# First product of the token groups in seven block products of eight, as the second one is, in a fused state space and PReLU kernel

## The chip, the cores and the metric

One core of a Trainium2 chip runs one program. The metric is the device time of one execution in microseconds (us), taken as the median over several executions. "Before" was run again beside every set of experiments, on the same chip: its medians were 415.87 to 416.51 us, except for the last set (415.48).

Engine names in the profile: PE is the matrix engine (TensorE), PEld its weight loads, DVE the VectorE, ACT the ScalarE, POOL the GpSimd.

## The reference

The first half is a state space scan over chunks of tokens; the second half, on which the change works, is two dense products with a PReLU between them.

```
def _moe_ref(x, w_in, w_out, alpha):
    h = x @ w_in                                         # 3072x256 @ 256x2048
    g = np.maximum(h, 0.0) + alpha * np.minimum(h, 0.0)
    return (g @ w_out).astype(np.float32)                # 3072x2048 @ 2048x256

def reference(**kwargs):
    ...                                                  # state space part, chunk by chunk
    attn_out = _attn_ref(**attn_kwargs)                  # (4, 8, 768, 32)
    x = np.ascontiguousarray(attn_out.transpose(0, 2, 1, 3)).reshape(B * S, H * D)
    return _moe_ref(x=x, **moe_kwargs)
```

All is float32. In the profile one float32 matmul leaves two records.

## The kernel before

Tokens go in six groups of 512. Group 0 is worked off with the weight loading; groups 1 to 5 form the main loop. The 2048 hidden units are 16 tiles of 128. For each tile, `hidden` multiplies 512 tokens by the two halves of the input and makes the PReLU from the PSUM bank: ScalarE writes `alpha*h`, VectorE takes the maximum with `h`.

```
def hidden(g, f, t0, nt):
    ...
    for k in range(KC):                                  # KC = 2
        nc.tensor.matmul(hp, w_in[:, k, f * P : (f + 1) * P], xts[g][:, k, t0 : t0 + nt],
                         start=(k == 0), stop=(k == KC - 1))
    gt = gts[g, f][:, t0 : t0 + nt]
    nc.scalar.mul(gt, hp, s_alpha[:, f : f + 1])
    nc.vector.scalar_tensor_tensor(out=gt, in0=hp, scalar=s_mul[:, f : f + 1], in1=gt,
                                   op0=ALU.mult, op1=ALU.max)
```

The second product is already in seven block products of eight (a Strassen-Winograd scheme). GpSimd makes the four differences of hidden blocks (`hidden_sums`, 256 elements each), TensorE runs the seven products into four banks (`products`), and one group later `combine` adds the seven results up:

```
def combine(g):
    ...
    nc.vector.tensor_tensor(out=c[0][:, 0], in0=m[2], in1=sa[:, 0], op=ALU.add)
    nc.vector.tensor_tensor(out=u[:, 0], in0=m[6], in1=sa[:, 0], op=ALU.add)
    nc.vector.tensor_tensor(out=u[:, 1], in0=m[7], in1=u[:, 0], op=ALU.add)
    nc.gpsimd.tensor_tensor(out=u4[:, 0], in0=u[:, 0], in1=sa[:, 1], op=ALU.add)
    ...
    nc.vector.tensor_tensor(out=c[0][:, 1], in0=m[3], in1=u4[:, 0], op=ALU.add)
```

The state space part is a generator, `pair`, whose steps are spread between the tiles. Its pieces:

```
bn = pair_loads(gp)                     # GpSimd: B times the decays, wanted by the state update
...
nc.vector.tensor_tensor_scan(out=dv[:, k], data0=abc[k], data1=ident_h, ...)   # 1024 elements
...
# state update: TensorE bn x xt, then VectorE `state`, GpSimd `sm`
for k in range(2):                      # gram products: two ss banks each, freed by VectorE masks
    gram = [ss_tile() ... for r in range(2)]
    ... nc.tensor.matmul(gram[r], bh[rs, k], cz[rs, :, k], ...)
    ... nc.vector.tensor_tensor(out=dec[:, k, hs], in0=gram[r], in1=dec[:, k, hs], op=ALU.mult)
    yield
```

The main loop goes through pairs of tiles; `products` run two pairs behind `hidden`.

Of the kernel before, what the change touches and what calls it, by code (L numbers as in the profile page):

```python
# [9 lines left out]
F32 = mybir.dt.float32  # L10
U32 = mybir.dt.uint32
U16 = mybir.dt.uint16
ALU = mybir.AluOpType
# [9 lines left out]
def kernel(  # L23
# [21 lines left out]


    nc = tc.nc
    ctx.enter_context(tc.manual_schedule(engines={
# [5 lines left out]
    P = 128  # L54
    Q = 128
    CPB = S // Q
    R = S // P
    NCH = batch * CPB
    HD = H * D
    RW = batch // 2 * H * CPB  # L60
    d_model, d_ff = moe_w_in.shape
    KC = d_model // P
    NF = d_ff // P
    GC = 4
    GT = GC * Q
    NG = NCH // GC
    NP = NCH // 2
    LAG = 2
    NQ = NF // 2
    HM = d_model // 2  # L70
    HT = GT // 2
    NB = 2
    WQ = 256
    assert H * N == P and HD == d_model and KC == 2 and R == CPB == 6
    assert NCH % GC == 0 and GT == 512 and NF % 2 == 0 and d_model <= WQ

# [4 lines left out]
    wld = ctx.enter_context(tc.tile_pool(name="wld", bufs=6))  # L81
    wtp = ctx.enter_context(tc.tile_pool(name="wtp", bufs=2))
    lda = ctx.enter_context(tc.tile_pool(name="lda", bufs=3))
    ldx = ctx.enter_context(tc.tile_pool(name="ldx", bufs=3))
    work = ctx.enter_context(tc.tile_pool(name="work", bufs=2))
    xtp = ctx.enter_context(tc.tile_pool(name="xtp", bufs=2))
    gp = ctx.enter_context(tc.tile_pool(name="gp", bufs=16))
# [179 lines left out]
    xts = {}  # L267
# [80 lines left out]
    def pair(gp):  # L348
# [7 lines left out]
        def decays(k):  # L356
# [5 lines left out]
            for w, t in enumerate(ahead.pop(k, None) or spread(z, k)):  # L362
                ws = slice(512 * w, 512 * w + 512)
                nc.vector.tensor_tensor_scan(out=dv[:, k, ws], data0=t, data1=ident_h[:, ws],  # L364
                                             initial=0.0, op0=ALU.mult, op1=ALU.add)

        ahead = {}
        if not abc:
# [28 lines left out]
        nc.scalar.copy(out=bh.rearrange("p k t -> p (k t)"), in_=tp[:, : 2 * P])  # L397
        cz = work.tile([P, 4, 2, Q], F32, name="cz")
        for e in range(4):
            nc.scalar.mul(cz[:, e].rearrange("p k t -> p (k t)"), ct, par[:, e : e + 1])  # L400
        if gp == 0:
# [6 lines left out]

        if gp:
            decays(0)  # L410
            yield
            decays(1)
# [27 lines left out]
        masked[b] = st[-1]  # L440
        yield


# [56 lines left out]

    def output(f):

        if f == 0:
            pos[0] = [bank(i).rearrange("p (t m) -> p t m", t=2) for i in range(GC // 2)]
        gt = gts.pop((0, f))
        for t in range(GC):
            nc.tensor.matmul(pos[0][t // 2][:, t % 2], gt[:, t * Q : (t + 1) * Q], w_out[:, f],  # L507
                             start=(f == 0 and t % 2 == 0), stop=(f == NF - 1),
                             skip_group_check=True)
        if f == NF - 1:  # L510
            for i, po in enumerate(pos.pop(0)):
                o_sb = op.tile([P, 2, d_model], F32, name="o_sb")
                nc.scalar.copy(out=o_sb, in_=po)
                t0 = 2 * i * Q
                nc.sync.dma_start(
                    out=out[t0 : t0 + 2 * Q, :].rearrange("(s p) m -> p s m", p=Q), in_=o_sb)
# [3 lines left out]
    wq = w_out.rearrange("p (q j) (i m) -> p q j i m", j=2, i=2)  # L520
    sums = []

    def weight_sums(q):
        if not sums:
            sums.extend(wld.tile([P, NQ, HM], F32, name=f"ws{i}", tag="raw") for i in range(3))
        a11, a12, a21, a22 = wq[:, q, 0, 0], wq[:, q, 1, 0], wq[:, q, 0, 1], wq[:, q, 1, 1]
        s1, s2, s4 = (t[:, q] for t in sums)
        for o, x0, x1, f in ((s1, a21, a22, ALU.add), (s2, s1, a11, ALU.subtract),
                             (s4, a12, s2, ALU.subtract), (a21, a11, a21, ALU.subtract)):
            nc.gpsimd.tensor_tensor(out=o, in0=x0, in1=x1, op=f)  # L530

    tsums = {}

    def hidden_sums(g, q):

        b11, b12 = (gts[g, 2 * q][:, h * HT : (h + 1) * HT] for h in range(2))
        b21, b22 = (gts[g, 2 * q + 1][:, h * HT : (h + 1) * HT] for h in range(2))
        ta = gp.tile([P, 2, HT], F32, name="gt")
        tb = gp.tile([P, 2, HT], F32, name="gt")
        t1, t3, t2, t4 = ta[:, 0], ta[:, 1], tb[:, 0], tb[:, 1]  # L540
        for o, x0, x1 in ((t1, b12, b11), (t3, b22, b12), (t2, b22, t1), (t4, t2, b21)):
            nc.gpsimd.tensor_tensor(out=o, in0=x0, in1=x1, op=ALU.subtract)  # L542
        s1, s2, s4 = (t[:, q] for t in sums)

        tsums[g, q] = [(1, wq[:, q, 0, 0], b11), (2, wq[:, q, 1, 0], b21), (6, s2, t2),
                       (5, s1, t1), (7, wq[:, q, 0, 1], t3), (4, wq[:, q, 1, 1], t4), (3, s4, b22)]

    ms = {}
    HALVES = {1: (0, 0), 2: (0, 1), 6: (1, 0), 7: (1, 1), 4: (2, 0), 3: (2, 1), 5: (3, 0)}

    def products(g, q, which):
        if q == 0 and which[0] == 0:
            ms[g] = [bank(i).rearrange("p (h t) -> p h t", h=2) for i in range(4)]
        for j in which:
            n, w, b = tsums[g, q][j]
            i, h = HALVES[n]
            nc.tensor.matmul(ms[g][i][:, h], w, b, start=(q == 0 and h == 0),  # L557
                             stop=(q == NQ - 1), skip_group_check=True)

    ends_of = {}  # L560

    def combine(g):

        m = {n: ms[g][i][:, h] for n, (i, h) in HALVES.items()}
        sa = wtp.tile([P, 2, HT], F32, name="sa", tag="wt")
        u = wtp.tile([P, 2, HT], F32, name="u", tag="wg")
        u4 = wtp.tile([P, 2, HT], F32, name="u4", tag="wr")
        c = [work.tile([P, 2, HT], F32, name=f"c{i}") for i in range(2)]
        last = g == NG - 1
        engs = [nc.sync, nc.scalar]  # L570
        nc.scalar.copy(out=sa[:, 0], in_=m[1])
        nc.scalar.copy(out=sa[:, 1], in_=m[5])
        nc.vector.tensor_tensor(out=c[0][:, 0], in0=m[2], in1=sa[:, 0], op=ALU.add)
        nc.vector.tensor_tensor(out=u[:, 0], in0=m[6], in1=sa[:, 0], op=ALU.add)
        nc.vector.tensor_tensor(out=u[:, 1], in0=m[7], in1=u[:, 0], op=ALU.add)
        nc.gpsimd.tensor_tensor(out=u4[:, 0], in0=u[:, 0], in1=sa[:, 1], op=ALU.add)
        nc.vector.tensor_tensor(out=c[1][:, 0], in0=u[:, 1], in1=m[4], op=ALU.subtract)
        nc.gpsimd.tensor_tensor(out=c[1][:, 1], in0=u[:, 1], in1=sa[:, 1], op=ALU.add)
        if last:
            turn(g, 0, c[0], slice(0, HT), engs)  # L580
            turn(g, 1, c[1], slice(0, GT), engs)
        nc.vector.tensor_tensor(out=c[0][:, 1], in0=m[3], in1=u4[:, 0], op=ALU.add)
        ms.pop(g)
        if last:
            turn(g, 0, c[0], slice(HT, GT), engs)
        else:
            ends_of[g] = c
# [12 lines left out]

    def finish(g):
        for i, c in enumerate(ends_of.pop(g)):
            turn(g, i, c, slice(0, GT), [nc.sync])

    pairs = {}

    def ssm(gp, stages=1):

        if gp not in pairs:
            pairs[gp] = pair(gp)  # L610
        for i in range(stages):
            next(pairs[gp], None)
# [5 lines left out]
    for i in range(3, 6):  # L618
# [10 lines left out]
    second = {0: (2, 1), 1: (2, 1), 2: (2, 1), 3: (2, 1), 5: (2, 1), 6: (3, 1), 7: (3, 1),  # L629
              8: (3, 1), 9: (3, 1), 11: (3, 1), 13: (3, 1)}  # L630
    for n in range(2):
        for f in range(NF):
# [15 lines left out]
            if n and f >= LAG:  # L648
                output(f - LAG)
    early[0] = None  # L650

    steps = {0: (1, 1), 1: (1, 1), 2: (1, 0), 3: (1, 0), 4: (1, 1), 5: (1, 1), 6: (1, 0), 7: (1, 0)}
    for i in range(NQ * (NG - 1)):
        g, q = divmod(NQ + i, NQ)
        nxt = 2 * g + 2 + q // 4
        if q % 4 == 0 and nxt < NP:
            if nxt == 4:
                load_rows(1)
                held["pr"] = rows_scan(1)
                rows_out(1)  # L660
            if nxt + 1 < NP:
                load_pair(nxt + 1)
        if i < NQ:
            weight_sums(i)
        for j in range(2):
            if steps[q][j] and nxt < NP:
                ssm(nxt)
            hidden(g, 2 * q + j, 0, GT)
            if i == 0:
                output(NF - LAG + j)  # L670
            elif i >= LAG:
                products(*divmod(NQ + i - LAG, NQ), range(4) if j == 0 else range(4, 7))
        hidden_sums(g, q)
        if g > 1 and q == LAG - 1:
            combine(g - 1)
        if g > 1 and q == LAG:
            finish(g - 1)

    for q, which in ((6, (0,)), (7, (0,)), (6, (1,)), (7, (1,)), (6, (3,)), (7, (3,)),
                     (6, (2, 4, 5)), (7, (2, 4, 5)), (6, (6,)), (7, (6,))):  # L680
        products(NG - 1, q, which)
    combine(NG - 1)


# [28 lines left out]
```

## Time and profile before

The four runs of the kernel before gave 415.72 to 416.1 us. A "wait" below is idle time of TensorE that the profile puts down to another engine. In the table, the granted clock is the share of full speed that TensorE got, averaged over the profiled execution.

| | before |
|---|---|
| median time | 415.96 us |
| profiled span | 413.6 us |
| TensorE busy | 392.2 us (95%) |
| VectorE, ScalarE, GpSimd busy | 212.6, 124.0, 216.7 us |
| mean granted clock | 0.994 |
| share of PE in the chain that ended last | 85% |

### The profile page before, as it was taken

To read this page: it belongs to the slowest core of one execution; us is meant where nothing else is said; L and a number is where in the kernel's file an instruction comes from. 1 tells how busy PE (TensorE), PEld (TensorE's weight loads), DVE (VectorE), ACT (ScalarE), POOL (GpSimd) and SP (SyncE) were. 2 spreads that over 40 slices of the span, in tenths; PEclk is the share of its full clock that TensorE was granted. 3 is DMA by queue.
4 is the path that set the end of the run, shared out by engine and by line. 5 is a ranking of instruction groups with operands and counts; after the bars stand their busy time and mean duration, and the time that the engine had idled before them with its cause. 6 is when DMAs were issued, how large, how long until landed. Compare 5 with 4: busy or idle time off the path is not lost.

```text
span 413.6 us, 5226 instructions
## 1 busy us (share of the span) xinstructions
PE 392.2 (95%) x1891; PEld 251.1 (61%) x1891; DVE 212.6 (51%) x322; ACT 124.0 (30%) x248; POOL 216.7 (52%) x267
## 2 busy tenths in 40 slices
PE   5878789999999999999999999999999999999993
PEld 4454558778556566566566566556556556666672
DVE  5999893852833732762732752731852731252223
ACT  3564824413223114124114124114123112221120
POOL 3244673450786965754734744734744824363441
PEclk9999999999999999999999999999999999999997
DMA  9939994100960610107810106920102000011003
GB/s 214 256 102 236 292 213 91 56 2 10 219 113 0 122 45 0 52 0 117 182 33 2 51 0 103 174 56 0 51 2 52 2 1 0 2 22 30 0 2 51
DMA packets 124122, 30.53 MB, mean 74 GB/s; under 512 B 96880, under 2 KB 120000, under 8 KB 124096
## 3 DMA queue, kind: packets, MB, share of 16 engines
q1 hardware_dynamic: 117792, 29.67, 32.1%
q10 hardware_dynamic: 6304, 0.52, 1.1%
q8 instruction: 15, 0.25, 0.2%
q14 instruction: 11, 0.09, 0.1%
HBM read 26.85 MB, written 3.34 MB: 73 GB/s over the span
## 4 chain that ended last, share of the span: by engine, by line
PE 85%; DVE 8%; POOL 3%; ACT 1%; DMA 1%; issue 1%; POOLq 0%; DVEq 0%
PE hp L494 37%; PE bank L557 28%; PE bank L507 7%; PE ss L448 5%; PE ss L471 2%; DVE dec L364 2%; DVE wr L221 1%; DVE dec L453 1%; PE ss L393 1%; PE ss L464 1%; PE ss L422 1%; DVE gt L498 1%; PE bank L342 1%; DVE dec L359 1%; DMA ap<-in_a_dram 1%
## 5 line engine op out<-in xcount | busy, mean ns | idle before, releaser
L542 POOL TENSOR_TENSOR gt<-gt 128x256 f32<-128x256 f32 x160 | 143.0, 905 | 140.5 <-DVE gt L498 118.7
L494 PE MATMUL hp<-xT,w_in 128*128 128x512 f32 (+1 forms) x416 | 179.4, 554 | 4.4 <-DVE gt L498 4.3
L498 DVE SCALAR_TENSOR_TENSOR gt<-hp,s_mul,gt 128x512 f32<-128x512 f32 (+1 forms) x104 | 71.4, 687 | 144.2 <-ACT gt L497 144.2
L497 ACT ACTIVATE gt<-hp,s_alpha 128x512 f32<-128x512 f32 (+1 forms) x104 | 66.7, 641 | 222.6 <-PE hp L494 185.8
L494 PEld LDWEIGHTS hp<-xT,w_in 128*128 128x128 f32 x416 | 74.8, 190 | 66.4 <-issue 53.3
L557 PEld LDWEIGHTS bank<-gt,w_out 128*128 128x128 f32 x320 | 60.8, 190 | 40.7 <-issue 36.1
L557 PE MATMUL bank<-gt,w_out 128*128 128x256 f32 x320 | 82.0, 379 | 0.0
L557 PE MATMUL bank<-gt,ws 128*128 128x256 f32 x240 | 64.7, 379 | 0.0
L557 PEld LDWEIGHTS bank<-gt,ws 128*128 128x128 f32 x240 | 45.6, 190 | 6.2
L359 DVE TENSOR_TENSOR_SCAN dec<-abc,ident_h 128x1024 f32<-128x1024 f32 x20 | 47.9, 2395 | 0.0
L453 DVE TENSOR_TENSOR dec<-ss,dec 128x512 f32<-128x512 f32 x40 | 25.7, 684 | 12.0 <-PE ss L448 12.0
L507 PE MATMUL bank<-w_out,gt 128*128 128x256 f32 x128 | 30.2, 379 | 0.0
L507 PEld LDWEIGHTS bank<-w_out,gt 128*128 128x128 f32 x128 | 24.3, 190 | 4.2 <-issue 1.0
L448 PE MATMUL ss<-cz,bh 64*128 64x512 f32 x80 | 24.3, 640 | 0.4 <-DVE cd L406 0.4
L224 POOL TENSOR_TENSOR w_out<-wr,wg 128x512 uint32<-128x512 uint32 x8 | 13.9, 1736 | 11.7 <-DVE wr L221 9.1
L400 ACT ACTIVATE cz<-ss,par 128x256 f32<-128x256 f32 x48 | 18.9, 484 | 0.0
L224 POOL TENSOR_TENSOR w_in<-wr,wg 128x512 uint32<-128x512 uint32 x7 | 8.9, 1272 | 13.6 <-DVE wr L221 13.6
L406 DVE TENSOR_TENSOR cd<-ss,ap 128x256 f32<-128x256 f32 x10 | 4.2, 424 | 20.1 <-ACT cz L400 20.1
L195 POOL TENSOR_SCALAR wt<-wt 128x512 f32<-128x512 f32 x15 | 11.3, 751 | 5.9 <-ACT wt L193 4.8
L437 POOL TENSOR_TENSOR sm<-state,bmask 128x256 f32<-128x256 f32 (+1 forms) x12 | 7.6, 637 | 10.4 <-DVE state L433 10.4
L448 PEld LDWEIGHTS ss<-cz,bh 64*128 64x128 f32 x80 | 6.9, 184 | 10.0 <-issue 6.1
L221 DVE SCALAR_TENSOR_TENSOR wr<-wt,wr 128x512 uint32<-128x512 uint32 x16 | 11.1, 693 | 2.4 <-POOL wt L195 1.0
(92 smaller groups left out, 249.3 us busy)
## 6 DMA issues: line engine op xcount, KB each, us to landing
abc<-z SPq DMA_DIRECT2D x20, 512.0 KB
raw<-in_moe_w_in_dram SPq DMA_DIRECT2D x8, 512.0 KB
raw<-in_moe_w_out_dram SPq DMA_DIRECT2D x8, 512.0 KB
xt<-in_x_dram SPq DMA_DIRECT2D x24, 128.0 KB
out_dram<-o_sb SPq DMA_DIRECT2D x34, 64.0 KB
nat<-in_B_dram SPq DMA_DIRECT2D x22, 64.0 KB
nat<-in_C_dram SPq DMA_DIRECT2D x22, 64.0 KB
ap<-pf SPq DMA_DIRECT2D x10, 128.0 KB
```

The source lines that it names most:

```text
L221: nc.vector.scalar_tensor_tensor(out=r, in0=t, scalar=3, in1=r, op0=ALU.logical_shift_left, op1=ALU.bitwise_xor)
L224: add.tensor_tensor(out=d, in0=r, in1=g.bitcast(U32), op=ALU.add)
L359: nc.vector.tensor_tensor_scan(out=dv[:, k], data0=abc[k], data1=ident_h, initial=0.0, op0=ALU.mult, op1=ALU.add)
L400: nc.scalar.mul(cz[:, e].rearrange("p k t -> p (k t)"), ct, par[:, e : e + 1])
L448: nc.tensor.matmul(gram[r].rearrange("p h t -> p (h t)"), bh[rs, k], cz[rs, :, k], start=True, stop=True, tile_position=(64 * r, 0), skip_ ...
L453: nc.vector.tensor_tensor(out=dec[:, k, hs], in0=gram[r], in1=dec[:, k, hs], op=ALU.mult)
L494: nc.tensor.matmul(hp, w_in[:, k, f * P : (f + 1) * P], xts[g][:, k, t0 : t0 + nt], start=(k == 0), stop=(k == KC - 1))
L497: nc.scalar.mul(gt, hp, s_alpha[:, f : f + 1])
L498: nc.vector.scalar_tensor_tensor(out=gt, in0=hp, scalar=s_mul[:, f : f + 1], in1=gt, op0=ALU.mult, op1=ALU.max)
L507: nc.tensor.matmul(pos[0][t // 2][:, t % 2], gt[:, t * Q : (t + 1) * Q], w_out[:, f], start=(f == 0 and t % 2 == 0), stop=(f == NF - 1), s ...
L542: nc.gpsimd.tensor_tensor(out=o, in0=x0, in1=x1, op=ALU.subtract)
L557: nc.tensor.matmul(ms[g][i][:, h], w, b, start=(q == 0 and h == 0), stop=(q == NQ - 1), skip_group_check=True)
```

## The change

The intent is to save an eighth of TensorE's time in the first product of groups 1 to 5 too. The tiles are taken by fours (a "quad", two pairs of tiles). A quad needs seven block products on 256 tokens, gathered in only two PSUM banks, `A` and `Y`, with ScalarE copies in and out. Below, M1 to M7 are the seven products of a quad by their block numbers; P1 to P7 are the second stage's products of the quad before, placed between them; `after(j)` marks the places at which other work is put in. The order in a quad is M1 (A), M5 (Y), M6 (A), M7 (A), M3 (Y), M4 (A), M2 (Y).

```diff
+    def prelu(o, h, z, i):
+        for p in range(2):
+            f = 4 * z + 2 * p + i
+            nc.scalar.mul(o[:, p], h[:, p], s_alpha[:, f : f + 1])
+            nc.vector.scalar_tensor_tensor(out=o[:, p], in0=h[:, p], scalar=s_mul[:, f : f + 1],
+                                           in1=o[:, p], op0=ALU.mult, op1=ALU.max)
+    def quad(g, z, after):
...
+        first(A, lambda q: wi[:, q, 0, 0], b11, True)           # M1
+        nc.scalar.copy(out=m1, in_=A)
+        after(1)
+        first(Y, lambda q: s1[:, q], t1, True)                  # M5
+        nc.scalar.copy(out=m5, in_=Y)
+        after(2)
+        after(3)
+        first(A, lambda q: s2[:, q], t2)                        # M6
+        nc.scalar.copy(out=u2, in_=A)
+        after(4)
+        after(5)
+        nc.vector.tensor_tensor(out=Y, in0=Y, in1=u2, op=ALU.add)
+        after(6)
+        first(A, lambda q: wi[:, q, 1, 0], t3)                  # M7
+        nc.vector.tensor_tensor(out=c22, in0=A, in1=m5, op=ALU.add)
+        after(7)
+        first(Y, lambda q: s4[:, q], b22)                       # M3
+        prelu(g12, Y, z, 0)
+        nc.scalar.copy(out=Y, in_=m1)
+        prelu(g22, c22, z, 1)
...
+        nc.gpsimd.tensor_tensor(out=tc_, in0=g22, in1=g12, op=ALU.subtract)
+        after(10)
+        first(A, lambda q: wi[:, q, 1, 1], t4)                  # M4
+        prelu(g21, A, z, 1)
+        after(11)
+        first(Y, lambda q: wi[:, q, 0, 1], b21)                 # M2
+        prelu(g11, Y, z, 0)
+        for o, x0, x1 in ((ta, g12, g11), (tb, g22, ta), (td, tb, g21)):
+            eng = nc.vector if g == NG - 1 and z == NZ - 1 and o is not td else nc.gpsimd
+            eng.tensor_tensor(out=o, in0=x0, in1=x1, op=ALU.subtract)
```

In step with it, the state space part is cut finer for the later pairs: half scans of 512 elements, and nine steps for six. The combine is cut into four parts that are placed in the first quad of the next group.

```diff
+        def half_decays(k, w):
+            ws = slice(512 * w, 512 * w + 512)
+            nc.vector.tensor_tensor_scan(out=dv[:, k, ws], data0=abc[k][:, ws], ...)
...
+    steps = {(0, 1): 0, (0, 2): 0, (0, 3): 0, (0, 4): 0, (0, 10): 0, (0, 13): 0,
+             (1, 1): 0, (1, 3): 0, (1, 6): 0,
+             (1, 10): 1, (1, 13): 1, (2, 1): 1, (2, 2): 1, (2, 4): 1, (2, 10): 1,
+             (3, 1): 1, (3, 3): 1, (3, 6): 1}
+    places = {3: 1, 5: 2, 6: 3, 9: 5, 10: 7, 13: 6, 14: 4}
...
+            if g > 1 and z == 0 and j in (5, 9, 13, 14):
+                ...                                             # next part of combine(g - 1)
+            if g > 1 and z == 1 and j in (4, 5):
+                finish(g - 1, j - 4)                            # output transposes
```

The sums of weight blocks (GpSimd, once) and of token blocks (GpSimd, four of 256 elements a group) are added as well.

## The prediction

> **What bounds the kernel now.** I read four views in this order: the page's busy shares and slices, the table of stretches, the groups by form, and the timeline of single stretches. From the page:
>
> ```profile
> PE 392.2 (95%) x1891; PEld 251.1 (61%) x1891; DVE 212.6 (51%) x322; ACT 124.0 (30%) x248; POOL 216.7 (52%) x267
> ...
> PE   5878789999999999999999999999999999999993
> ```
>
> TensorE is full from about 60 us on; the other engines are half idle. The table of stretches (busy us of PE, PEld, DVE, ACT, POOL) shows the same after the start:
>
> ```profile
> 164.00:228.00 64.00, 64.00 (x300) 39.27 (x300) 31.83 (x43) 17.14 (x34) 35.00 (x40) 1.00 0.32 62
> ```
>
> So the main loop (token groups 1 to 5, from 101.4 us, where the chain shows its first 512-column matmul, to 406.9 us) is TensorE's instruction stream without holes. The chain of waits gives the price of its pieces: four records of the first product (`hp`, 512 columns; each fp32 matmul leaves two records) take 1.72 us, eight records of block products (256 columns) 1.73 us. A matmul of 512 columns costs 0.86 us, one of 256 columns 0.43, exactly half, even with new weights each time. Below I call 0.86 us a unit, U.
>
> In the chain the same half group recurs at 169.09, 200.28 and 231.47 us: a group with two pairs of state space work takes 62.4 to 62.8 us, and one without (group 5, eight steps of 6.46) 51.7.
>
> The durations that I need, from the groups by form:
>
> ```profile
> L497 ACT ACTIVATE gt<-hp,s_alpha 128x256 f32<-128x256 f32 x24 | 11.5, 481 | 27.5 <-PE hp L494 27.4
> L498 DVE SCALAR_TENSOR_TENSOR gt<-hp,s_mul,gt 128x256 f32<-128x256 f32 x24 | 11.4, 477 | 14.2 <-ACT gt L497 14.1
> L359 DVE TENSOR_TENSOR_SCAN dec<-abc,ident_h 128x1024 f32<-128x1024 f32 x20 | 47.9, 2395 | 0.0
> ```
>
> and from the timeline, for GpSimd beside VectorE:
>
> ```profile
> 227.86 2.28 DVE L359 TENSOR_TENSOR_SCAN dec<-abc,ident_h 128x1024 f32<-128x1024 f32 x1
> 228.08 2.57 POOL L542 TENSOR_TENSOR gt<-gt 128x256 f32<-128x256 f32 x1 [0.71 <-DVE gt L498]
> ```
>
> That GpSimd subtraction takes 0.72 us elsewhere; begun inside a scan it ends 0.5 us after it. [...]
>
> [...] VectorE's `cd` reads the same bank as ScalarE's `cz`, needs nothing from it, and waits 20.1 us in all for it (nine times). [...]
>
> **The change part by part.** *Removed:* the first product of a group was 16x2 matmuls of 512 columns, 32 U = 27.5 us. It becomes four quads of seven products of two 256-column matmuls, 28 U = 24.1 us. Saved 3.44 us a group, 17.2 us in five groups: 398.7 us if nothing is given back. State space work, second products and the last transfers keep their TensorE time.
>
> *Added, beside TensorE:* per quad three 512-element ScalarE copies out of PSUM and one into it, two VectorE adds, eight PReLU halves instead of four whole ones, four 512-element GpSimd subtractions. Sums: ScalarE about 6.3 of 12 us, VectorE 5.2 plus the state space's, GpSimd 4x1.27 (the 512-element add of the weight conversion takes 1.27). No engine becomes full. The weight sums (GpSimd, 16x1.27) fall mostly into 75 to 100 us, where GpSimd is half idle. What counts is the waits.
>
> *(a) The lockstep.* The built program, whose waits can be read without running it, has both PSUM banks of a quad reused by the next quad, and lets the second half of a PReLU on ScalarE wait for VectorE's first half, as they share a bank. Three of the four PReLUs read PSUM. Take a quad without state space work, with the end of product 3 (bank Y) at 0; ScalarE starts 0.26 after TensorE goes on (285.13 to 285.39 in the timeline), VectorE 0.03 after ScalarE, and I take 0.05 for ScalarE after VectorE. First PReLU: 0.26 + 4x0.48 + gaps = 2.29. Copy into Y (0.59, as the `o_sb` copy): 2.94. TensorE meanwhile has P5, P7, M4, 3 U = 2.58, so M2 waits 0.4. ScalarE's two halves from SBUF: 3.8. Third PReLU in lockstep to 5.88, which frees bank A; TensorE stands at 5.63. Fourth PReLU: 7.42, which frees Y; the next M5 would have come at 6.8. From M5 to the end of the next product 3 are 7 U = 6.03 of TensorE. Sum 13.5 us a quad, against 14 U = 12.06 of work and 12.92 before. Group 5 gives back 4x1.45 = 5.8. With state space work TensorE's inserts (about 10.8 us a group) fill some of these holes, but in the first and third quad a half scan (1.14) stands in VectorE's queue between second and third PReLU and lengthens the loop. Worked out quad by quad in the same way I get holes of 1.5, 1.5, 1.5 and 1.1: 5.6 a group, 22.4 in four. Together 28 us.
>
> *(b) The combine.* VectorE's last combine add waits for `u4` on GpSimd, which now stands behind three 512-element subtractions that begin only after the fourth PReLU: 3x1.27 + 0.73, plus up to 1.14 under a scan. Behind that add stand, in VectorE's queue, the masks of the first gram product; the second gram product needs their two banks. TensorE would be there some 2.4 us after the fourth PReLU and gets the banks after about 6.5: 3.5 to 4.5 us in groups 2, 3 and 4. In group 5 the add into Y stands there instead: 2 us. About 14 us.
>
> *(c) The state update.* At a group's start `bn` (0.64) stands on GpSimd behind the last quad's three subtractions: ready 4.6 us after the fourth PReLU, later with the two half scans. TensorE wants it 2.7 us after. 2 to 4 us in groups 2, 3, 4: about 9.
>
> Sum: 398.7 + 28 + 14 + 9 = 450. The holes of (b) and (c) let ScalarE and VectorE catch up, so parts of (a) are counted twice, and the 0.05 gaps may be shorter: I take off a sixth of the 51, about 8.
>
> **The rivals.** *TensorE stays full and 17 us are gained (399 to 405 us).* For it: no engine is overloaded, and the placing of the products looks as if tuned; the slack at each bank is missed by only 0.4 to 0.7 us, so much shorter ScalarE or VectorE times would do it. Against it: 0.48 us is the measured mean, and four in a row is no choice of a scheduler. *Gain and holes cancel (about 410 to 420):* this would be (a) half as large with (b) and (c) hidden. (b) and (c) follow from queue order alone, so I give it little. *GpSimd becomes the bound:* its sum is about 30 of 60 us a group with the sums and the state space; only its latency matters. *More start-up:* seven weight sums in group 0 could delay the weight conversion, whose GpSimd add is on the chain at places; they come after the steps that need it, so I put below 2 us on it.
>
> **Range and chances.** 442 us. The low end, 418, is (a) at half size and (b), (c) at a third; the high end, 460, is the full sum plus weight loads exposed at each restart (0.19 each). A gain of 2% needs all holes to stay under 9 us, which only a wrong reading of the lockstep gives; but somebody placed these steps with care, so I leave 0.12 for it. Within 2%: 0.08. Slower: 0.80.
>
> **What would show it.** Right: TensorE busy falling below 90% in the slices after 100 us; its idle time put down to VectorE's PReLU (before M1 and M5), to ScalarE's copy into Y (before M2), to the masks (before the second gram product of a group) and to GpSimd `bn`; quads of about 13.5 us in group 5; VectorE's last combine add with an idle time of several us after GpSimd. Wrong: TensorE at 95% or more and quads of 12.1 us, then the lockstep costs nothing; or PReLU halves well under 0.48 us; or no VectorE wait on `u4`. Units for 256 columns other than 0.43 us would upset the saving itself.

The sum came to 398.7 + 28 + 14 + 9 = 450, less 8 for double counting, so 442 us. The text rests on two things. That engines sharing a bank are made to wait for each other stood in the built program, and the trace of before has the 20.1 us of `cd` behind `cz` for it. That each engine works in the order in which its instructions were issued was my assumption; the trace of after bears it out in this place: VectorE stood idle for 2.80 us until the combine's add at 274.45, and ran the masks issued behind it only at 274.79, though their gram product had ended at 269.68. The 1.14 us of a half scan in (a) and (b) is half of a whole one's 2.28; the trace of after has 1.22. The 0.19 us in the range is the mean weight load of before (190 ns); that each restart exposes one was an estimate.

## More of the kernel before

The clock by slices, each a fortieth of the span (9 is 90% or more), is at its top nearly everywhere:

```profile
PEclk9999999999999999999999999999999999999997
```

## The result and the profile after

The kernel after takes 472.84 us (472.08 to 474.27, four runs), before 415.96. The ratio is 1.137, 95% interval 1.134 to 1.140. Ratios here are the mean time of one kernel's fast runs over the mean of the other's fast runs in the same rounds, so not quite the ratio of the medians that I quote.

The loss is 57 us where I had predicted 26, and 472.84 lies outside my range of 418 to 460. From the page of the kernel after, the busy times and the slices that answer to those shown of before:

```profile
PE 406.8 (86%) x2131; PEld 302.9 (64%) x2131; DVE 269.5 (57%) x460; ACT 183.8 (39%) x408; POOL 217.6 (46%) x189
...
PE   6778899996998978599897869998859989989994
...
PEclk9999799999799998979998989999897999999998
```

The first line holds the puzzle. TensorE has 17 us less work than before and is busy for 14.6 us *longer* (406.8 against 392.2). The third line holds a part of the answer: the clock falls in slices that were at the top before, mostly near a slice with a low busy share. Mean clock: 0.954, against 0.994.

First the waits. TensorE's waits by who ended them (total us, times, longest us):

```profile
PE hp L616 <- DVE gt L601: 13.6, 21, 2.8
PE ss L476 <- DVE dec L481: 11.8, 3, 3.9
PE ss L445 <- POOL bn L327: 10.6, 4, 3.4
...
PE hp L616 <- ACT hp L645: 4.2, 16, 1.0
```

These are the three waits of the prediction, by name. Line 616 is the quad's matmul: it waits for the PReLU half on VectorE (21 times), and for the copy into Y (16 times). Line 476 is the second gram product, three times, up to 3.9 us. Line 445 is the state update, which waits for `bn`.

*The lockstep*, from the timeline of group 4's last quad (start, length, engine, operation; in square brackets the idle time before it and what ended it):

```profile
398.96 0.46 ACT L600 ACTIVATE gt<-hp,s_alpha 128x256 f32<-128x256 f32 x1
...
399.50 0.48 DVE L601 SCALAR_TENSOR_TENSOR gt<-hp,s_mul,gt 128x256 f32<-128x256 f32 x1
...
400.01 0.84 ACT L600 ACTIVATE gt<-hp,s_alpha 128x256 f32<-128x256 f32 x2 [0.59 <-DVE gt L601]
```

ScalarE's second half begins when VectorE's first half has ended (399.98), though it needs nothing from it; both read one bank. The PReLU of `c22`, which lies in SBUF, shows no such wait: its two ScalarE halves take 0.91 us in one go at 398.15. In group 5, which has no state space work, the quads follow each other after 13.3 to 13.4 us, except for one of 15.8. I take such periods from one quad's copy into Y to the next's.

*The combine*, in the timeline of group 3's first quad:

```profile
269.00 4.74 POOL L659 TENSOR_TENSOR gt<-gt 128x512 f32<-128x512 f32 x3 [1.90 <-DVE gt L601]
...
273.70 0.72 POOL L686 TENSOR_TENSOR u<-u,sa 128x256 f32<-128x256 f32 x1
...
274.45 0.42 DVE L692 TENSOR_TENSOR c<-bank,u 128x256 f32<-128x256 f32 x1 [2.80 <-POOL u L686]
274.79 1.28 DVE L481 TENSOR_TENSOR dec<-ss,dec 128x512 f32<-128x512 f32 x2
...
275.53 2.21 PE L476 MATMUL ss<-cz,bh 64*128 64x512 f32 x4 [3.93 <-DVE dec L481]
...
277.67 2.07 PE L616 MATMUL hp<-xs,ws 128*128 128x256 f32 x4
```

GpSimd works off the quad's three subtractions, then `u4`; VectorE's last add waits for it; behind it in VectorE's queue stand the masks; behind the masks TensorE has stood still for 3.93 us. And the next product of the quad, four records of 256 columns, takes 2.07 us, twice its usual 1.03.

*The state update*, at the start of the same group:

```profile
254.35 0.64 POOL L327 TENSOR_TENSOR bn<-nat,prt 128x256 f32<-128x256 f32 x1
...
255.04 0.44 PE L445 MATMUL ss<-xt,bn 128*64 128x128 f32 x4 [3.38 <-POOL bn L327]
255.41 1.38 PE L592 MATMUL bank<-gt,w_out 128*128 128x256 f32 x4
...
256.58 1.91 PE L592 MATMUL bank<-gt,ws 128*128 128x256 f32 x4
...
258.29 1.66 PE L616 MATMUL hp<-xs,w_in 128*128 128x256 f32 x4
259.79 1.03 PE L616 MATMUL hp<-xT,ws 128*128 128x256 f32 x4
```

TensorE stands for 3.38 us, and what it does next is slow. Four records of 256 columns are 1.03 us where TensorE runs on at full clock (the next four start after 0.86, so the ends overlap), and 1.10 to 1.13 as the first after a stop; here they are 1.38, 1.91 and 1.66 before the usual 1.03 comes back. The table of stretches shows the same with the granted clock beside it. Its columns are the stretch, its length, busy us of PE, PEld, DVE, ACT and POOL with their instructions, then the clock, the DMA share and GB/s:

```profile
252.00:256.00 4.00, 0.96 (x7) 0.74 (x8) 1.68 (x2) 0.50 (x2) 2.95 (x4) 1.00 0.39 106
256.00:260.00 4.00, 4.00 (x12) 3.21 (x11) 1.04 (x3) 0.37 (x1) 0.41 (x1) 0.57 0.08 25
...
272.00:276.00 4.00, 0.47 (x1) 0.29 (x2) 1.55 (x3) 0.00 (x0) 3.02 (x4) 1.00 0.00 0
276.00:280.00 4.00, 4.00 (x10) 2.17 (x9) 2.67 (x5) 0.22 (x1) 0.00 (x0) 0.58 0.00 0
```

After each of the two holes there are 4 us in which TensorE is "busy" throughout at 0.57 or 0.58 of its speed. Cut at its edges, 256.14:259.55, the table gives 0.50: the clock is halved for 3.41 us. The trace has seven such stretches in the main loop, four of 3.41 and three of 6.83 us. So such a hole is paid for twice: once as idle time, and once as busy time that does half the work. That second part is in no line of waits, and it is one reason why the busy time went up.

It is not the only one. Against a TensorE with 17.2 us less work, the busy time is 31.8 us too long, of which the clock explains 13.7 (see e1_fill). The profile also counts as busy what a restart costs: behind each stop the ends of the last records no longer overlap with the next ones (1.03 - 0.86 = 0.17 us), and the first four records take up to 0.1 longer. In e7_pairwise, with the same operations and the same clock of 0.954, the stops over 0.03 us after 105 us fall from 46 to 22 and the busy time falls by 6.9 us (406.8 to 399.9), of which 1.5 is clock. From this and the two lengths above I estimate 0.2 to 0.3 us a stop, or 10 to 13 us for 46 stops.

The trace has these stretches behind the six holes of 3.37 to 3.94 us in groups 2 to 4. But the stretch at 0.50 in group 1, from 116.20 to 123.02, goes with a hole of only 2.77 us, and the hole of 1.52 us at 421.38 has none. The prediction had no term for any of it.

### The profile page after: what moved, and what is told of

Its sections match the earlier page's. It is cut to its first block, busy times and chain, and to the rows that moved or that the text cites. A ratio compares the mean times of both kernels' runs of the same rounds, so it can differ in the third digit from the quotient of the medians.

```text
span 470.4 us, 5917 instructions
## 1 busy us (share of the span) xinstructions
PE 406.8 (86%) x2131; PEld 302.9 (64%) x2131; DVE 269.5 (57%) x460; ACT 183.8 (39%) x408; POOL 217.6 (46%) x189
## 4 chain that ended last, share of the span: by engine, by line
PE 49%; DVE 22%; ACT 13%; POOL 10%; issue 4%; DMA 1%; POOLq 0%; ACTq 0%; DVEq 0%
PE hp L616 15%; PE bank L592 13%; DVE gt L601 12%; ACT gt L600 9%; POOL gt L659 7%; PE bank L535 5%; PE ss L476 4%; PE hp L522 4%; ACT hp L645 2%; DVE dec L375 2%; DVE dec L481 2%; PE ss L499 2%; DVE dec L370 1%; POOL xs L575 1%; PE ss L445 1%
## 5 line engine op out<-in xcount | busy, mean ns | idle before, releaser
L659 POOL TENSOR_TENSOR gt<-gt 128x512 f32<-128x512 f32 x58 | 91.2, 1572 | 36.1 <-DVE gt L601 25.4
L650 POOL TENSOR_TENSOR gt<-gt 128x512 f32<-128x512 f32 x20 | 32.1, 1603 | 136.4 <-DVE gt L601 121.7
L600 ACT ACTIVATE gt<-hp,s_alpha 128x256 f32<-128x256 f32 x120 | 54.5, 472 | 91.8 <-DVE gt L601 41.7
L601 DVE SCALAR_TENSOR_TENSOR gt<-hp,s_mul,gt 128x256 f32<-128x256 f32 x120 | 55.9, 480 | 48.3 <-ACT gt L600 48.2
L592 PEld LDWEIGHTS bank<-gt,w_out 128*128 128x128 f32 x320 | 62.6, 198 | 11.8 <-issue 1.5
L616 PE MATMUL hp<-xT,w_in 128*128 128x256 f32 x160 | 45.7, 409 | 15.4 <-DVE gt L601 11.2
L375 DVE TENSOR_TENSOR_SCAN dec<-abc,ident_h 128x512 f32<-128x512 f32 x32 | 50.3, 1593 | 0.0
L616 PE MATMUL hp<-xs,ws 128*128 128x256 f32 x160 | 47.3, 421 | 2.4 <-DVE gt L601 2.4
L616 PEld LDWEIGHTS hp<-xT,w_in 128*128 128x128 f32 x160 | 27.7, 192 | 31.8 <-DVE gt L601 18.4
L616 PEld LDWEIGHTS hp<-xs,ws 128*128 128x128 f32 x160 | 30.1, 203 | 24.0 <-issue 10.5
L616 PE MATMUL hp<-xs,w_in 128*128 128x256 f32 x160 | 42.5, 389 | 0.0
L476 PE MATMUL ss<-cz,bh 64*128 64x512 f32 x80 | 28.2, 722 | 13.5 <-DVE dec L481 11.8
L481 DVE TENSOR_TENSOR dec<-ss,dec 128x512 f32<-128x512 f32 x40 | 25.8, 685 | 18.4 <-PE ss L476 18.4
L616 PEld LDWEIGHTS hp<-xs,w_in 128*128 128x128 f32 x160 | 30.0, 193 | 5.4 <-issue 1.6
L633 ACT COPY u<-hp 128x512 f32<-128x512 f32 x20 | 11.8, 592 | 49.4 <-PE hp L616 49.4
L522 PE MATMUL hp<-xT,w_in 128*128 128x256 f32 x96 | 27.6, 412 | 3.8 <-DVE gt L526 3.8
```

The lines of the kernel that those rows point to most:

```text
L375: nc.vector.tensor_tensor_scan(out=dv[:, k, ws], data0=abc[k][:, ws], data1=ident_h[:, ws], initial=0.0, op0=ALU.mult, op1=ALU.add)
L476: nc.tensor.matmul(gram[r].rearrange("p h t -> p (h t)"), bh[rs, k], cz[rs, :, k], start=True, stop=True, tile_position=(64 * r, 0), skip_ ...
L592: nc.tensor.matmul(ms[g][i][:, h], w, blocks[g, z][n][:, p], start=(q == 0 and h == 0), stop=(q == NQ - 1), skip_group_check=True)
L600: nc.scalar.mul(o[:, p], h[:, p], s_alpha[:, f : f + 1])
L601: nc.vector.scalar_tensor_tensor(out=o[:, p], in0=h[:, p], scalar=s_mul[:, f : f + 1], in1=o[:, p], op0=ALU.mult, op1=ALU.max)
L616: nc.tensor.matmul(to[:, p], w(2 * z + p), b, start=start and p == 0, stop=True, skip_group_check=True)
```

## The experiments

Twelve kernels ran, all correct against the reference. Line numbers shift by a few between them. The ratios use the runs of before of the same set. "Clock" is the mean granted clock of the profiled execution.

| run | median us | ratio to before | clock |
|---|---|---|---|
| after | 472.84 | 1.137 | 0.954 |
| e1_fill | 459.11 | 1.104 | 0.988 |
| e2_u4 | 462.09 | 1.111 | 0.960 |
| e3_bn | 456.08 | 1.096 | 0.970 |
| e4_evac | 450.52 | 1.082 | 0.955 |
| e5_all | 428.89 | 1.031 | 0.967 |
| e6_scan | 414.24 | 0.995 | 0.982 |
| e7_pairwise | 447.97 | 1.076 | 0.954 |
| e8_coarse | 478.91 | 1.149 | 0.935 |
| e9_best | 410.11 | 0.987 | 0.989 |
| e10_bestpw | 419.84 | 1.010 | 0.995 |
| e11_hole0 (on before) | 437.13 | 1.053 | 0.991 |
| e12_hole4 (on before) | 480.64 | 1.156 | 0.946 |

My theory was: the three waits of the prediction (lockstep, combine, `bn`), plus a drop of the clock behind the long ones, as the trace of after has it behind the holes of 3.37 to 3.94 us. The rivals: the clock is an accompaniment and not a cost; another wait stands behind the three; the nine steps of the state space part are to blame.

The theory of e11_hole0 was that a short hole costs its own length alone, and that of e12_hole4 that a long one costs 1.5 to 3 us more, an estimate from some 14 us for the seven or eight holes of the kernel after.

### The clock: fill the holes without shortening them (e1_fill)

Matmuls with zero weights are put into the two long holes, where TensorE would stand. The waits of all other engines stay as they are.

```diff
-        dps = ss_tile().rearrange("p (k m) -> p k m", m=P)
+        dps = ss_tile()
+        for _ in range(7 if fine and gp >= 6 and gp % 2 == 0 else 0):
+            nc.tensor.matmul(dps[:, : 2 * Q], zeros, ident_h[:, : 2 * Q], start=True, stop=True, ...)
+        dps = dps.rearrange("p (k m) -> p k m", m=P)
...
+            if 1 < g < NG - 1 and (z, j) == (1, 3):
+                for _ in range(8):
+                    nc.tensor.matmul(ms[g][0][:, 0], zeros, ident_h[:, :HT], start=False,
+                                     stop=False, ...)
```

> The changed kernel with seven zero-weight matmuls (3.0 us) before the state update of the first pair of groups 2 to 4 and eight (3.4 us) before their second gram product, that is inside the two holes of 3.37 and 3.93 us. The waits stay; TensorE only has work in them. Clock theory [...]: the clock stays near 1 behind the holes and the time falls by 10 to 14 us, to 459 to 463, with the quads from the first to the second of groups 2 to 4 at about 23 us in place of 25.3. Rival (only the waits cost, the lower clock lies beside waits anyway): 472 to 474, no change.

Measured: 459.11 us, 13.7 us less than after, clock 0.988. The bank waits have not moved at all:

```profile
PE hp L620 <- DVE gt L605: 13.6, 21, 2.8
```

Work was *added* to TensorE, no dependency was removed, and the kernel became 13.7 us faster. The clock records say the same: of the seven stretches at 0.50, the six in groups 2 to 4 are gone, 27.3 us in all, and half of that is 13.7. The one of group 1 (6.83 us) is still there. So the clock drop costs at least 13.7 us, and 459 us is what the waits and the restarts, with at most 3 us of clock, make of the kernel.

### The price of a hole by itself (e11_hole0, e12_hole4)

The same question asked in the kernel before, where nothing of the change is present. Ten times in the main loop TensorE waits for the PReLU of the tile it has just finished, by one small added matmul on that result, directly (n = 0) or after a chain of four ScalarE copies (n = 4).

```diff
+    def hole(t, n):
+        for i in range(n):
+            o = holes.tile([P, GT], F32, name="ho")
+            nc.scalar.copy(out=o, in_=t)
+            t = o
+        nc.tensor.matmul(ss_tile()[:, :P], t[:, :P], zeros, start=True, stop=True)
...
             hidden(g, 2 * q + j, 0, GT)
+            if q in (2, 6) and j == 1:
+                hole(gts[g, 2 * q + j], n)
```

> The price of a hole by itself, in the kernel before: ten times in the main loop, 31 us apart, TensorE waits for the PReLU of the hidden block that it has just finished (one added matmul on that result), holes of some 1.8 us. Theory [...]: +16 to +20 us, 432 to 437 us, clock 0.98 or more. Rival (any hole lowers the clock): above 442 us.

> The same ten holes lengthened by a chain of four ScalarE copies (0.58 us each), to some 4.1 to 4.4 us. As bare idle time they would cost +40 to +45 us: 456 to 462 us (rival: the holes alone). Theory [...]: +56 to +75 us, 472 to 492 us, and the mean clock 0.95 or less.

Measured: 437.13 us with the short holes, a hair beyond what I expected, clock 0.991; 480.64 with the long ones, clock 0.946. The waits (total, times, longest), first of the short holes, then of the long ones:

```profile
PE ss L620 <- DVE gt L499: 17.0, 10, 1.7
```

```profile
PE ss L620 <- ACT ho L618: 42.2, 10, 4.2
```

With short holes the time rose by 437.13 - 415.48 = 21.7 us: 17.0 of waiting, and 4.6 for ten added matmuls of 0.46. Only 0.1 is left over. With long holes it rose by 65.2: 42.2 of waiting and the same 4.6 leave 18.4 us, 1.8 per hole. The clock takes them: behind each of the ten holes the trace has a stretch at 0.50, eight of 3.41 and two of 6.83 us, and with short holes it has none in the main loop. The records just behind one hole of either kind show it, short hole first:

```profile
256.25 0.46 PE L620 MATMUL ss<-zeros,gt 128*128 128x128 f32 x2 [1.71 <-DVE gt L499]
256.54 1.03 PE L558 MATMUL bank<-gt,w_out 128*128 128x256 f32 x4
257.41 0.59 PE L558 MATMUL bank<-gt,ws 128*128 128x256 f32 x2
```

```profile
276.74 0.49 PE L620 MATMUL ss<-zeros,ho 128*128 128x128 f32 x2 [4.22 <-ACT ho L618]
277.06 1.53 PE L558 MATMUL bank<-gt,w_out 128*128 128x256 f32 x4
278.38 1.06 PE L558 MATMUL bank<-gt,ws 128*128 128x256 f32 x2
```

The same six records of block products take 1.5 us behind the short hole and 2.4 behind the long one. The rival, that any hole lowers the clock, falls with the first kernel; the rival, that a hole costs its length, falls with the second.

That every shorter hole leaves the clock alone is not shown, though. The traces of the other runs have drops behind some: in e2_u4 behind two of three holes of 2.45 us (stretches at 0.50 from 199.57 and 346.35; the next four records of 256 columns take 1.95 and 2.07 us, behind the third hole 1.13), and in e8_coarse four times behind a hole of 1.6 us with a shorter one beside it (from 143.42, 221.93, 300.43 and 378.94, each 3.41 us long). In all runs every hole of 2.58 us or more in the main loop had a drop; those between 1.6 and 2.45 us had one in some places and none in others (none at 2.13 in e10_bestpw). What decides there stays open.

### The combine's add on VectorE (e2_u4)

```diff
-        nc.gpsimd.tensor_tensor(out=u4, in0=u[:, 0], in1=sa[:, 1], op=ALU.add)
+        nc.vector.tensor_tensor(out=u4, in0=u[:, 0], in1=sa[:, 1], op=ALU.add)
```

> The changed kernel with one edit: the combine's add u4 runs on VectorE in place of GpSimd, so that VectorE no longer waits behind GpSimd's three subtractions. My step (b): the 3.93 us wait before the second gram product goes in groups 2, 3, 4, with it its share of the low clock (about 8 us), and 1.5 us in group 5: 449 to 455 us. Rival (VectorE is late at the masks because of its own work, scans and PReLU): the wait only moves to the masks themselves, above 467.

Measured: 462.09 us, 10.8 less than after. That is neither what the theory expected nor the rival. VectorE's wait for GpSimd is gone, yet TensorE still waits for the masks, 7.4 us in all where it was 11.8. VectorE's own queue is late:

```profile
267.21 4.83 POOL L659 TENSOR_TENSOR gt<-gt 128x512 f32<-128x512 f32 x3 [1.90 <-DVE gt L601]
...
267.77 0.99 DVE L686 TENSOR_TENSOR u<-u,sa 128x256 f32<-128x256 f32 x1
...
268.69 2.29 DVE L375 TENSOR_TENSOR_SCAN dec<-abc,ident_h 128x512 f32<-128x512 f32 x1
...
270.90 0.39 DVE L689 TENSOR_TENSOR c<-u,bank 128x256 f32<-128x256 f32 x1
271.21 0.41 DVE L692 TENSOR_TENSOR c<-bank,u 128x256 f32<-128x256 f32 x1
```

The `u4` add and the half scan read two operands from SBUF, beside GpSimd's subtractions, which began before them. The add takes 0.99 us (0.42 in e9_best, at 401.52), and the half scan, one of those that the change put here, 2.29 us (1.22 a little earlier, at 263.03, where GpSimd's subtraction began after it and took 2.12 us instead of 1.27). The two combine adds that read a bank, beside the same subtractions, take 0.39 and 0.41. The wait behind GpSimd hid a second one behind VectorE.

### `bn` a quad earlier (e3_bn)

The pair's generator gets a stop after `bn`, and that first step is issued in the last quad of the group before, ahead of its subtractions.

```diff
         bn = pair_loads(gp)
+        if gp >= 2 * GC // 2:
+            yield
...
-                ssm(nxt + steps[z, j])
+                k = nxt + steps[z, j]
+                ssm(k, 1 if k in pairs else 2)
+            if nxt + 2 < NP and (z, j) == (3, 8):
+                ssm(nxt + 2)
```

> The changed kernel with bn of a group's first pair issued on GpSimd already in the last quad of the group before, ahead of that quad's subtractions. My step (c): the 3.37 us wait before the state update goes in groups 2, 3, 4 with its share of the low clock (about 5 us): 456 to 460 us, and the quads from last to first at 14.5 to 15 us in place of 19.2. Rival (the state update would then wait for something else, the second SSM bank or the input transfers): above 467.

Measured: 456.08 us, 16.8 less than after, clock 0.970. The period from a group's last quad to the next group's first fell from 19.2 to 14.2 us. A hole of 3.38 us was removed three times, about 10 us, and 17 us came back: a hole is worth more than its length here too, 2.2 us more by the time and 1.6 by the period (5.0 - 3.4).

### The lockstep (e4_evac, e7_pairwise)

In e4_evac ScalarE copies the bank to SBUF first, and both halves of the PReLU read the copy; the bank is free after 0.58 us. In e7_pairwise no operation is added: the two ScalarE halves are issued before the two VectorE halves.

```diff
-        prelu(g12, Y, z, 0)
+        h12 = evac(Y)                        # nc.scalar.copy into an SBUF tile
         nc.scalar.copy(out=Y, in_=m1)
+        prelu(g12, h12, z, 0)
...
-        prelu(g21, A, z, 1)
+        prelu(g21, evac(A), z, 1)
...
-        prelu(g11, Y, z, 0)
+        prelu(g11, evac(Y), z, 0)
```

> The changed kernel with each PSUM PReLU preceded by a 512-element ScalarE copy of the bank into SBUF, on which the PReLU then works, 1.8 us more ScalarE work a quad; the banks come free after 0.59 us in place of 2.0. My step (a), lockstep: the waits before M1, M5 and M2 go, quads of group 5 fall from 13.3 to 12.1 us, and the time falls by 18 to 25 us to 448 to 455, the two long holes staying. Rival (ScalarE's extra work takes the place of the lockstep, or the waits are the products' and not the banks'): quads of group 5 stay above 13 us, 468 to 480.

```diff
-        for p in range(2):
-            f = 4 * z + 2 * p + i
+        fs = [4 * z + 2 * p + i for p in range(2)]
+        for p, f in enumerate(fs):
             nc.scalar.mul(o[:, p], h[:, p], s_alpha[:, f : f + 1])
+        for p, f in enumerate(fs):
             nc.vector.scalar_tensor_tensor(out=o[:, p], in0=h[:, p], ...)
```

> The kernel after with both ScalarE halves of a PReLU issued before both VectorE halves: no ScalarE half waits for a VectorE half any more, but VectorE's first half waits for ScalarE's second. Theory of the lockstep: a PReLU from PSUM costs 4 x 0.48 us in a row either way as to the bank's release, so the last PReLU ends no earlier, but ScalarE comes free one VectorE half earlier, in three places of a quad: 0.3 to 0.8 us a quad, with the clock some 8 to 20 us: 453 to 465 us. Rival (ScalarE's and VectorE's total work, not their alternation, sets the quad): no change, 470 to 475 us.

Measured: e4_evac 450.52 us, 22.3 less than after. In group 5 three of the four quads now follow each other after 12.08 to 12.15 us, and fourteen units of 0.86 are 12.06: without the lockstep a quad costs its TensorE work and nothing more. The new wait that shows is an old one, uncovered: TensorE comes earlier to the second gram product and waits there 15.2 us in all instead of 11.8.

e7_pairwise 447.97 us, 24.9 less than after, more than I expected (8 to 20). My working for it was too small. The last two of the four PReLUs of the same quad as shown above, in this kernel:

```profile
380.88 1.54 ACT L600 ACTIVATE gt<-hp,s_alpha 128x256 f32<-128x256 f32 x4
...
381.79 1.66 DVE L602 SCALAR_TENSOR_TENSOR gt<-hp,s_mul,gt 128x256 f32<-128x256 f32 x4 [0.30 <-ACT gt L600]
```

Their eight operations flow without a gap, ScalarE half a PReLU ahead of VectorE. In the kernel after, each ScalarE half stood 0.5 to 0.6 us for its VectorE neighbour. From the first half of a quad's PReLUs to the end of the last I read 5.8 us here against 6.8 in the kernel after. So one reordering of a few lines, without any operation more or less, takes back almost half of the loss.

### Is it the nine steps? (e8_coarse)

The quads stay; the state space part goes back to six steps and whole scans.

```diff
-        fine = gp >= 2 * GC // 2
+        fine = False
...
+    steps = {(0, 1): 0, (0, 2): 0, (0, 4): 0, (1, 1): 0, (1, 3): 0, (1, 6): 0,
+             (1, 10): 1, (1, 13): 1, (2, 2): 1, (3, 1): 1, (3, 3): 1, (3, 6): 1}
```

> The kernel after with the state space part in six steps, as in the kernel before, inside the new quads: whole scans [...] instead of halves. Theory (the waits come from the quads and the combine, and the nine steps soften them): same or slower, 465 to 480 us. Rival (the nine steps themselves cost the time, as the half scans stand at the end of the first quad): 455 us or less.

Measured: 478.91 us, 6 us more than after, clock 0.935. The rival falls: the finer steps help. The whole scans take 2.73 us here in the mean, 2.40 in the kernel before. TensorE's wait for `bn` alone is 17.4 us in this kernel, up to 5.6 at a time. GpSimd's `bn`, 0.64 us in the kernel after, here lies beside a whole scan and takes four times as long:

```profile
260.18 2.62 POOL L327 TENSOR_TENSOR bn<-nat,prt 128x256 f32<-128x256 f32 x1
```

In this respect the change's finer steps were well chosen.

### The three mends together, and the scan moved (e5_all, e6_scan)

e5_all is e2, e3 and e4 in one kernel.

> The three mends together: the u4 add on VectorE, bn issued a quad earlier, and a ScalarE copy of the bank to SBUF ahead of the three PReLUs that read PSUM. Theory (the three waits of the prediction, with the clock drop that they bring, are the whole loss): alone they gave 10.8, 16.8 and 22.3 us; if nothing else stands behind them most of that adds up, the wait before the second gram product alone stays in part (2.45 us in the second run), so 398.7 plus 3 groups x about 6 plus some 6 in groups 1 and 5: 412 to 428 us. Rival (a further wait, not in the prediction, stands behind these and takes their place): 435 us or more. If it lands under 408 it beats the kernel before.

Measured: 428.89 us, 44 less than after; the three alone gave 10.8 + 16.8 + 22.3 = 49.9. That is 0.9 us above what the theory expected. The rival of a further wait is not quite out of the field: the second gram product still waits 10.7 us, up to 3.2 at a time, for VectorE's masks.

e6_scan also moves the half scan that stood in front of the combine's last adds in e2_u4 to behind the first gram product's masks.

```diff
-            for w in range(2):
-                half_decays(1, w)
-                yield
+            half_decays(1, 0)
+            yield
...                                          # in the gram loop, after the masks:
+            if fine and k == 0:
+                half_decays(1, 1)
```

> As the run of the three mends together, and the last half scan of each pair (1.14 us alone, 2.29 beside a GpSimd subtraction), which stands in VectorE's queue just ahead of the combine's last adds, is put behind the masks of the first gram product. Theory (the wait before the second gram product is VectorE's own queue): 2 us shorter waits in groups 2, 3 and 4[...]: 5 to 12 us less than that run. Rival (the scan only moves the wait to the second gram product's masks, 1.1 to 2.3 us later): within 3 us of it.

Measured: 414.24 us, 14.7 less than e5_all (expected 5 to 12), clock 0.982 after 0.967. The wait for the masks, in e5_all and then in e6_scan:

```profile
PE ss L479 <- DVE dec L484: 10.7, 4, 3.2
```

```profile
PE ss L478 <- DVE dec L483: 3.2, 3, 1.1
```

7.5 us of waiting were removed and 14.7 us gained. Again about half of the gain has no wait to its name: the holes of 3.2 us became holes of 1.1, and the three stretches at 0.50 behind them, 17.1 us in all, are gone.

### A version that beats both (e9_best, e10_bestpw)

What TensorE still waited for in e6_scan is behind operations that need not stand where they stand. e9_best adds no operation. It issues the combine's last two parts behind the first gram product's masks, the output transposes behind the add into Y, and group 0's two output copies behind the first quad's PReLUs.

```diff
-            if g > 1 and z == 0 and j in (5, 9, 13, 14):
-                if j == 5:
+            if g > 1 and (z, j) in ((0, 5), (0, 9), (1, 4)):
+                if z == 0 and j == 5:
                     comb[0] = combine(g - 1)
                 next(comb[0], None)
-            if g > 1 and z == 1 and j in (4, 5):
-                finish(g - 1, j - 4)
+            if g > 1 and z == 1 and j in (6, 8):
+                finish(g - 1, j // 2 - 3)
             ...                              # state space step
+            if g > 1 and (z, j) == (1, 2):
+                next(comb[0], None)
```

> The three mends and the moved half scan (414.24 us, faster by half a per cent than before), and three more moves on VectorE and ScalarE, no operation added: the combine's last two parts issued after the masks of the first gram product; the two output transposes of a group moved from ahead of the second quad's add into Y to behind it; group 0's two output copies on ScalarE moved behind the PReLUs of group 1's first quad. Theory (what is left of the loss is these queue orders): the TensorE waits that the 414.24 us kernel still shows go, 3 x 1.06 before the second gram product, 1.57 + 0.45 + 2 x 0.3 behind the add into Y, some 0.85 of 1.78 in group 1: 6.7 us less, 406 to 409 us, about 2% under before. Rival (the moved work only meets the next deadline, the state space output product or the later PReLUs): 412 us or more.

e10_bestpw is e9_best with the pairwise order in place of the three copies.

> As the best version, but the pairwise order of the PReLU halves in place of the three ScalarE copies of the banks. Theory (the pitch of the PReLUs counts: pairwise order brings it from some 1.45 us to 0.9 as well, but the bank is held until VectorE has read it): slower than the best version by the difference of the quads that the two mends showed alone in group 5, 12.75 against 12.15 us for 14 units, so by up to 0.6 us a quad, in 20 quads at most 12: 409 to 421 us. Rival (ScalarE's added 20 us of copies cost as much as they save): equal or faster.

Measured: e9_best 410.11 us (four runs, 409.49 to 410.58) against 415.48 for before (415.01 to 416.93): ratio 0.987, interval 0.985 to 0.988. It beats both kernels, though by 1.3% and not by the 2% that I hoped for. All quads of group 5 now take 12.1 us. Part of the rival came true: the moved adds meet the next deadline, and a new wait of 0.8 us stands three times at the products' bank that they read last:

```profile
PE bank L596 <- DVE c L702: 2.5, 3, 0.8
```

e10_bestpw takes 419.84 us, as the theory expected: alone the pairwise order was worth more than the copies (24.9 against 22.3 us), in the mended kernel less. Its quads of group 5 take 12.4 to 12.7 us. That this comes from the bank, which is still held until VectorE has read it, is the theory; no run tests it apart.

A group with state space work takes 61.3 us in e9_best (13.6 + 17.3 + 13.9 + 16.5), where 62.6 - 3.44 = 59.2 is its TensorE work by my units. The waits listed account for about one of the two missing microseconds (0.83 and 0.31). The rest I have not traced.

## Why the prediction was wrong

**Units and saving: right.** Quads at 12.1 us in e4_evac and e9_best are the 14 U of 0.86 that I worked with.

**(a) The lockstep: right in mechanism and close in size.** The halves wait for each other as the built program said; group 5's quads came at 13.3 to 13.4 us, predicted 13.5. Both mends of it, one with copies, one by order alone, gave 22 and 25 us of the 28 predicted. TensorE's listed waits of this kind are only 18.4 us (13.6, 4.2 and 0.6 at the second stage's banks); the restarts are in no list.

**(b) The combine: right, and deeper than I saw.** The wait was 3.93 us in groups 2 to 4 (predicted 3.5 to 4.5) and 1.52 in group 5 (predicted 2). But I took `u4` on GpSimd as the cause. Moving it brought only 3.93 to 2.45: the half scan that I had counted only as a neighbour of the PReLUs stands in the same queue, stretched to twice its length. That is an error in the account of the cause which the sum did not show.

**(c) `bn`: right.** 3.38 us three times, predicted 2 to 4.

**The step that failed is the pricing of the holes.** In the prediction's sum, "398.7 + 28 + 14 + 9 = 450", each hole stands with its own length, and the range's high end added for restarts only "weight loads exposed at each restart (0.19 each)". The runs show what belongs there: behind each of the long holes of groups 2 to 4 (3.4 to 3.9 us) the clock falls to one half for 3.4 or 6.8 us. In the kernel after this cost 13.7 us (e1_fill), and in a kernel without any of the change 1.8 us per hole of 4.2 us, against nothing per hole of 1.7 us (e12_hole4, e11_hole0). My own (b) and (c) predicted six holes of 2 to 4.5 us; with 1.8 us each they would have said 11 us more. The profile of before could not show it: in its main loop, from 101.4 to 406.9 us, TensorE waited 0.2 us in all.

**A second, smaller error: the restarts.** I took off "a sixth of the 51, about 8" because the holes might let the other engines catch up. The waits themselves bear that out: in the lists the lockstep has 18.4 us, the combine 13.3 (11.8 and 1.5) and `bn` 10.6, together 42.3, where I had 51 and, with the discount, 43. But with the clock held up the kernel takes 459.1 us, 60.4 over 398.7. The 18 us beyond the listed waits are counted as busy: by the estimate above 10 to 13 are restarts, up to 3 are clock that was still lost (0.988 against 0.994 of some 457 us), and 2 to 5 stay open. I had restarts only in the high end, at 0.19 each. That 459.1 lies so close to this high end of 460 is luck: the waits were 9 smaller than I had them, and beside them stood 18 us where the high end had 10.

Put together: 398.7, + 42.3 of listed waits, + 18 beside them, + 13.7 for the clock is 472.7; measured 472.84. The 18 is a remainder, so this sum had to close. (The low end of the range adds up to 420 by its own terms, or 417 with the discount, not 418; nothing hangs on it.)

**The rivals.** TensorE full and 17 us gained: it would have needed the holes gone, and even the mended kernel of 410 us gets a third of the gain. Gain and holes cancel (410 to 420): not this kernel, but e6_scan. GpSimd as the bound: no, at 46% busy; only its latency counted, as I had said.

**The signs.** The busy share in the slices did fall; the releasers named were the right ones (VectorE's PReLU, the copy into Y, the masks, `bn`), and VectorE's last combine add idled 2.80 us and more after GpSimd. None of my signs looked at the granted clock.

## What to carry to other kernels

When a change is about to open holes in a matrix engine that was full, price each hole by its length, by 0.2 to 0.3 us for the restart (my estimate), and, if it may come to 2.58 us, from where every hole in these main loops had a drop, by about 2 us more for the half speed behind it (1.8 us a hole in e12_hole4, 13.7 us for six in e1_fill; shorter ones, down to 1.6 us, were hit in places); the profile shows these parts as busy time, so read the clock line beside the busy line. When two engines each work off halves of one bank, issue all of the first engine's halves before the second's (24.9 us in e7_pairwise), and look at what stands in a queue ahead of an operation that another engine waits for: reordering, three copies a quad and one add moved to another engine turned 14% slower into 1.3% faster. Mends uncover the waits behind them (the second gram product's went from 11.8 to 15.2 us in e4_evac), so look at the waits again after each.
